# Other places for a table and for the tiles of wo, and 99 operations at other positions of the stored order, in a kernel that mixes dilated attention and a spectral filter

## The chip, the cores and the metric

The kernel runs on one core of one Trainium2 chip. The metric is the device time in microseconds (us); the kernel before takes 453.42 us, the median of three runs (453.15 to 453.45).

## The reference

```python
# x: (1, 2048, 640); 32 heads of 20; 8 taps 2 apart, looking back only
qkv = (x @ wqkv)                                  # split into q, k, v per head
logits = einsum("bhsd,bhswd->bhsw", q, k[taps]) * scale     # masked where s - 2w < 0
a = einsum("bhsw,bhswd->bhsd", softmax(logits), v[taps]) @ wo
b = irfft2(rfft2(x) * (w_r + 1j * w_i), s=(2048, 640))
g = sigmoid((x * gate_w).sum(-1, keepdims=True))
out = g * a + (1 - g) * b
```

## The kernel before

The sequence is cut into 16 blocks of 128 rows, even rows ("xe") and odd rows ("xo") apart. The projection to q, k and v runs in groups of heads. A weight is loaded raw, cast on ACT to its high part and subtracted on DVE or POOL to get the low part, and PE multiplies the parts. The first weights are loaded as `st` tiles by ACT's own DMA queue. The sums (`ev`) go out to a buffer in DRAM (`qkvd`) and come back for attention as `kt`, `q` and `vt` in units called 0a, 0b up to 7b.

`attend` computes one such unit in four steps: `pr` = kt times q (a copy of q is made on ACT into one of three thirds of a PSUM bank, `qbank`, and DVE multiplies with it; some pieces are multiplied on POOL straight from q), a reduction into `L` (the logits, e.g. `L6a`), then maximum `m`, exponential on ACT, sum `s`, reciprocal. After that POOL multiplies `vt` with the weights into `pv`, and DVE reduces that into `o`, which is stored.

The spectral half is a two dimensional Fourier transform by matrix products. `freq(g)` treats one of 16 groups of frequencies in the order 1, 2, 3, 0, 4 to 15. PE makes `u` and `v` from `zc` and the table `bt`; ACT copies v to `vs`; DVE makes `ab` = u + vs and u - vs; PE makes `x` and `z` from ab and the table `mm`. ACT copies x into `P` and writes `X`, a signed copy of x and z, and two DMAs on ACT's queue carry its halves across the partitions into P. POOL multiplies P with the filter `wp` and adds two parts of it; DVE finishes `z`, then makes `s`; PE makes `g` from s, and ACT copies g into `zg`, which the later spatial stage (`oa`, `ob`, `ha`, `hb`) reads. Group 0 is special: it has a table of its own, `tbfirst`, and a second pair `ix`, `iz` instead of the exchange by DMA. The last stage multiplies the attention's output with wo (`woa`, `wob`, output `ya`); a transposed tile is `oTp` in PSUM and `oT` in SBUF. `load_wo` loads wo raw (`wor`), casts it on ACT and subtracts on POOL.

No scheduler orders the work. `Plan.record` collects every operation of every engine; `Plan.order` decodes a stored list of indices (`ORDER`, 99 of whose entries concern us here), takes the operations out one by one in that order, and `Plan.issue` issues them. Since each engine works through its own instructions in that order, an operation that must wait holds all that stands behind it on the same engine, DMA issues on ACT's and SP's queue included. Every instruction is therefore shown at line 385, the line on which the helper executes it, and tiles have to tell them apart.

Where a tile lies is fixed by its tag. `Ring` hands out tags in turn, and a tile with the tag of an earlier one may be written only when that one's readers are done. `x0` to `x7` first hold `st` tiles and then xo; `raw0` to `raw4` the raw weights and later zc, vs, X.

Of the kernel before, what the change touches and what calls it, by code (L numbers as in the profile page):

```python
# [201 lines left out]


ORDER = """
T>t<81poj4|NsC0{{R31`zHT%QmDPk&^9H>y=H*?`Lk%9Gnl%)B_CdQV7rLsIrdLM6sJFoVB8Rk|2U=URH5DLwHy3}>N|I2375U5sNENOZ_r>p;QjNS0Qt^d&3_BFn1BL!{U(U9<aW#`
(4{je$Bsor%a-5-0xjIIz5Bhxq2@_J(ZuU^ngytDZDQ}-t=xl(zWY*>f`~oBV87-{Mb^4R1miDSrW!ct$(P^W^D-my%k>BL--#k$dtRgI1R2eM!0IO6o?xU&oVN(ll5SwBMVENpPvsM&
VX`y5BH+<-e7!dXm4S)sH)6INBza7DP`fU`9t|k`wa4c^oeIq*)7CzRjTY+mf9&=qHQ*h+Q~~C@lecBhmUgi^3s$MljG$M^2A?T>032Y~xgI;PDn0`}JfpXlPl|zc84Qwq<`4=%Gxo}a
8aTyUW$<0lvv}Yi{qWtE5;ndiT9Il;=`-mwYQl}5l>T>2mc)1@SbB472vpebS-0G>xhr1`IH0OO^WWem*}=TuJ*N?b=-d(+YVg*L!??m3Sl>7Ow>k%WopAr_cs>TQ#{0e@C)rMmjvX42
HQ(%xOkCb5Ti|9M&74oX@)~%FC+g&Um>cIj7Th&a$THElCM_Qxh94S8@_R$YuH^AlZ29A62|gtX_GwKt861v*&%|Lj%A~%)Ju4ard*J9-%@(h(=zcz=9{hy8`{2ylZ=~+70?!1ipBf(&
zwb}8-f;L(FVHcuzwYP7?2%s*U{nv&ECs$KBfw^t@z;C&Xf&zSgn_WXO0Ra-A{p=`KSTo&WCxLcHX{frWWSucqtk!hm#2nHJeX5P<a5rX;@Kti_Yl8ko7HnBP?BD0BCR!|nSp+9pO(On  # L210
7C*Q$o$wOs&SmSBdiC|DHG?D8$uS*E_ccd=5LY{i^BiXwbd{r0)D57<l%^E2DaY|53+8~ZxRJddAoRNdJYPz%5Lvh5W}S={Qu`$OJ}cwneg)RxR)(xpZMXtIs%DRMvJ7u?%%!@^1B8h@
(qlVz@tLYv`rnaOHo>WRfe{k*SBQiEnDF!z+o6MsFAJ=(MehAC+OQk;gfj{$D4Y9E8C&GfcpM}t1W|C%hJ#;L!7aan3ZqicP~xB7_Qnrj(tTe<@R?W&V{($jS4EF-5t#TOP0?OuT|3Qa
eIT(hT>jCQrecqER6AALUaUC?)=4v!RW)w9%$6TmkX}rmdZ1<A!<Ce0_LGFT-55A$ndz>!p$dHdxh1>o=3<(6z*KuxX86ZbhMDSB?~D@~6mK>u#>!XP<ORCokbE-Ovd^FevYd6|yTLNh
6LqbJKy?z;o)=#fxd)}q(t!E7s4(3|QOszQKMHHgt&?pyfYSMq-!@LPp=HMQOrhAsZ-JWy-C3Mc^Z`{5!$bngKocKj*>1lOfpe>gL<4DAk0)0!w_E-I8Ix5zA0pAPHAB79wZiA}lY^=h
Std;TST@mvK(Izv+y2xl{ZkLjAJfK%G&=WMvx-dxg6DMA424jO9cS?4TWJptst&`UzGq$ZfJ_rYlV4K31$NLXrgHytE*H`DST?S8Z+_yEBRpdjK2A~uXM4Nj32C4N!P4z2;Hqn$;QEkU
x#r;cod7g-0_+HHSjTx0G?wMOQFZ}koI>bLqzm3R1#oY}9`o)-A1NE;d6CRy2FU=-R;2owOP)Xp5@L{{lo`pBpk%V|R6g=MDVwD`bNH=OjT}S9%<^i$H2}^WSgi-blEMMxNCWOt@KVe#
HqSpv<!^C>%lNmv7RSF7$EOxNC{yKe#`U(Lx+?J!T>!ZP9DRYha-KfY6f?D)z+1)BTY#H0H8P_on~L7A?2-f-TVGlJ$NYiPg`Ivs?eZmoz*1s%9Xd;!3V#C-+$0Brl2%!N#H_A1i{L@S
P#-7P*l5}1Q+W5C%(=qlbU3pZ%otQHBXliSa7Eq92vyz1<`-h2wlnrTN(?T$K{1wyGNT3yESJ?d;(Zw=a_uas{jBg++Q~Nj2jh-_=z=SgoGX(xs<sgT2K8=TN&l`u^j-}yWbYSO(5cEw
hVcGl#lx!tpndKnI3W6}4nYMD+Pk`P27A{L32W`ao5f1Lx*Nb1X()n(JDUZ2O2az;7O<uub@cq%>A*E(_tL!Qq_R=1wNX@G<vau7PJDCp_$;h81hHJ;PIGy_$BYC9!FRj&Q%d@dloNT&
V}(@XS$iJK7_UBeT9exaHe0ZCd>(H!PSGFR8O~kQ=y2V-@rw&$Jg2mnKHs;xrCurTIvRujMxI%zzSsUAbNQyk@KBwL05WxN*Sm)5I2Xq^XZjzH)Ihl#)t51ss6A^!b?3)adQa(X1?V`Q  # L220
wEf(@vgv8sXd>1A(Inx$aDsF9o|pp|HZf+o&w(aEY-(nPPdJX2mvN>(E_fL#$UQPvI|Oa9cnbzr-e$^;-WQD_g83Pq)JF@6puq4=iw_oAzI4h0IpY+hbO=V@zz#KK7T>Y)df*No_7zw#
J`ZNS1m5yd>sTzrvwN&$9|njAQz>w>cl%q7wQZn?8p!=9m>5`9rRfIf_1}m*K9QWX2p$bk-U|1B1Z(^)NFjGTUi*=`v=?z{hl`I|qiO|ofbK~N2V}%VS*t!h=6?gk(z$O~7sEFHmYj%6
MNgL}676SI+-J!42{U}iie@2JyD7wX?tWyweu6+;9xiJSQlECBlw3cU6JNL9Qbq$0tUe_bx^QVlnRQ^tl#ei^!;Uy@((9<|ywE43$z4IgNR)3HBAWp^wA5G)i`pF3l<h}x3OgiJc*rTp
yDIhR4d;b1#P9;B=Fn!{JagvZWQ8Dna+>C8?PWN5+e!O%eKQFD7&UwCI9EJuzf24eM=px5vm)*=iSJQOsoOrV0(&B;X_MREg42C+90%XRnO_)k_RRKzcw`jk&FlJtxyJ@dT+yf~v((s8
-2h}>WX&Km>`JDrIZsB~HyMCyj)w7Emh<Bxtc+@vJ<-~GPXyd<K2@BwUFJSEEbOSLf-}5Tj30C4oH>gKhj@`yM0lgO1I|~8Uz5d)n(Ap~u7*R$VC*4V^uL@BrFYVSXJ!#;GPx$-`iB^*
2MiYfr5xOz@(Hn_ZO=uraJXL7TjCH2Oo22&4b<5GbESU)fMy@w<%JD=kBRvs^7YntD5lPeG0~#A(Y7f~=u1vSN3y;*%B)if3ZHyCNgsIjl_GRnl%27NSP+9t2PA;2H4bS5GyaV=>j*#x
*M~~EY1!7%?esLp+*GX}o-QD6C&^J6=;H8X|6(A(`yZi}Z}faaS0?Gjqv@lj&ep&tv$=yAF_CROwlnc;Gg~`p{^9llwa}e7zb`&fYr`LIz+M4&!D;pBW0~8c-9pQAVK~5|Lst>X_XHJf
BbHYtz@n{+NemE;D#YqvNyi@TUL%=x!c}A)W#~0YXI_9y%G_JmIy7up9F-wz0Ko(;nI?_m?Kd3a(}245c2v@Jf1OP32?$)b@4&S%LtI4Xl7SDnL8i5%lEDj)>G1TqOFDWr8uzjy&O3Nm
d$+wYoEer$Aq-KST1DqGF`N6nbu3i9J1y!73cVHXcW7RCc*0zmf=AnkP~}&rJ5)<G5jD!ivtsQGa!*YrUZ<x(O%YP2uxAQgki#<4cU6)m;~U+_$c%HUxDD2C>6*du+*nLhT21G%FSMTx
F9o90(I?=4__Uh>X7zl2S;|3%g?xk&&ZNy<yz%i{Sl87#;Hq(*dX#-S;0K7k`-=_DNmtn_cWizA<)OfVpjTP3DV~JDA&$35ndX-;RJ~3efGwiJ5Ht%!mBpiuzqzwAm%V<N$YT+%N<y?-  # L230
L$<-n`T;@{9ha=_DU5Caogirb*l5ll(=hVGvPaUVHGn@TTk@(O%Cg>+!F&Z>^a}MWs*HoAIXZ*IGmD&KQ1$s5UlW<f%b`0L6Zo}XxY*ejMiL6wZB3VWksk25LDcc$*m+|kO*MiA5qM!R
E4&I$iUB%e=t-&vI#oE3omS`8qhKNa{&xtjquCoj@gt~4hPP`#R?lah{_Fr2NG)2)6j`)6xWw-bn!#53kreFmg|f%8{Hi9hP;wz{AL5rvcI#V0DymT1c(Kucy<*0`8=s--Bri8zDH~#v
%-FB#M0Qq%ICg_IFP2C48|n56Sm9Um9k2fiPvpqah%)KEUW1~=uV*6=QB*z{Al8lvW9Q;ye=6Tp=v>L79H5IQ5X|z~#8hpnJr+Ga_QrkC4`Rhv7#WXovCK>ybSs8B6l~NOoIP)O5Fr!S
+}fcYgLx<p#v>wbK=gW?vhdCXZVtgKhsHNHj%~Qolp5+lQ(hjj51#p5_1_2~j|^=(cHJD!9j9&qpZdcxvk%!cXv8;;W{9m%oyJFbB38c|mac656_T8#{}Kg@00
"""


# [729 lines left out]
```

## Time and profile before

| | |
|---|---|
| median of three runs | 453.42 us |
| profiled execution | 455.89 us |
| its span on the core | 454.1 us, 7249 instructions |
| mean granted TensorE clock | 0.996 |
| PE, DVE, POOL, ACT busy | 441.2, 409.8, 363.9, 211.9 us |
| moved by DMA | 110.75 MB, mean 244 GB/s |

The span is the time from the first to the last instruction of the profiled execution; 1.79 us of its 455.89 us lie around it. Busy times are those of arithmetic instructions, PE being TensorE's matmuls, PEld its weight loads, DVE VectorE, ACT ScalarE, POOL GpSimd, SP SyncE; ACTq and SPq are the DMA queues that those engines issue to. All times in the rows are counted from the start of the span. A group of like instructions is shown as one row with its start, its length and their number.

### The profile page before, as it was taken

The page shows a single profiled execution, that of the slowest core. Times are in us where ns is not written, and L with a number is a line of the kernel's source. Part 1 is how long each engine was busy: PE and PEld are TensorE (multiplying, and loading weights), DVE is VectorE, ACT ScalarE, POOL GpSimd, SP SyncE. Part 2 cuts the span into 40 slices and gives each one's busy share as a digit, 9 for nine tenths or more (in the row PEclk, how much of TensorE's full clock was granted, in tenths as well). Part 3 has the DMA queues.
Part 4 walks back from the last instruction along what each step waited for, and adds up shares of the span by engine and source line. Part 5 has one row for each costly group of instructions (what it writes and reads, how often), then busy time and mean ns, then how long its engine had stood idle before and what let it go on. Part 6 is the DMA issues. An engine that isn't in the chain of part 4 may idle for free. (4 is left out here: it accounts for less than half of the span.)

```text
span 454.1 us, 7249 instructions
## 1 busy us (share of the span) xinstructions
PE 441.2 (97%) x2440; PEld 391.8 (86%) x2440; DVE 409.8 (90%) x519; ACT 211.9 (47%) x561; POOL 363.9 (80%) x316
## 2 busy tenths in 40 slices
PE   9999999999999999999998989999989999999996
PEld 6888888888889888899886769998877899999996
DVE  4899999899999999999978989999999997899484
ACT  4723165625226463255356666667554655342110
POOL 1158895899899898988977898976899998889810
PEclk9999999999999999999998999999999999999999
DMA  8998999887968979679979778989883331365932
GB/s 312 401 383 268 340 330 377 305 264 237 272 183 272 340 217 316 181 216 320 303 220 294 240 230 250 297 245 320 258 257 105 85 97 54 118 207 134 296 123 87
DMA packets 73956, 110.75 MB, mean 244 GB/s; under 512 B 21296, under 2 KB 50992, under 8 KB 73920
## 3 DMA queue, kind: packets, MB, share of 16 engines
q1 hardware_dynamic: 40192, 69.32, 46.8%
q10 hardware_dynamic: 32816, 36.97, 26.1%
q0 software_dynamic: 912, 4.00, 2.4%
q8 instruction: 19, 0.31, 0.3%
q14 instruction: 17, 0.14, 0.1%
HBM read 72.51 MB, written 32.84 MB: 232 GB/s over the span
## 5 line engine op out<-in xcount | busy, mean ns | idle before, releaser
L385 PE MATMUL qkv<-w,xo 128*128 128x480 f32 (+1 forms) x480 | 110.6, 385 | 0.0
L385 PE MATMUL qkv<-w,xe 128*128 128x480 f32 (+1 forms) x474 | 104.3, 382 | 0.0
L385 PEld LDWEIGHTS qkv<-w,xe 128*128 128x128 f32 x474 | 89.3, 189 | 15.2 <-ACT xe L385 0.9
L385 PEld LDWEIGHTS qkv<-w,xo 128*128 128x128 f32 x480 | 89.7, 189 | 13.8 <-ACT zg L385 0.2
L385 ACT COPY ev<-qkv 128x480 f32<-128x480 f32 x64 | 34.9, 558 | 48.3 <-PE qkv L385 35.9
L385 PE MATMUL woa<-wo,oT 128*128 128x320 f32 x240 | 47.2, 318 | 0.4 <-ACT oT L385 0.4
L385 PE MATMUL wob<-wo,oT 128*128 128x320 f32 x240 | 46.9, 315 | 0.2 <-ACT ya L385 0.2
L385 POOL TENSOR_TENSOR P<-P,wp 128x963 f32<-128x963 f32 (+1 forms) x16 | 35.4, 2212 | 6.6 <-DMA P<-X 4.0
L385 PEld LDWEIGHTS woa<-wo,oT 128*128 128x128 f32 x240 | 37.7, 188 | 1.1 <-ACT oT L385 0.6
L385 PEld LDWEIGHTS wob<-wo,oT 128*128 128x128 f32 x240 | 37.8, 188 | 0.6 <-ACT ya L385 0.4
L385 POOL TENSOR_TENSOR fx<-fx 128x160 f32<-128x160 f32 (+1 forms) x16 | 12.8, 818 | 24.2 <-DMA fc<-in_t_fc 17.1
L385 POOL TENSOR_TENSOR w<-raw,w 128x480 fp32r<-128x480 f32 (+1 forms) x20 | 24.8, 1262 | 5.3 <-ACT w L385 5.3
L385 ACT CAST oT<-oTp 128x384 fp32r<-128x384 f32 (+1 forms) x32 | 13.4, 427 | 30.9 <-PE oTp L385 17.3
L385 PEld LDWEIGHTS g<-mm,s 128*128 128x128 f32 x150 | 21.0, 190 | 7.1 <-ACT zg L385 5.0
L385 PE MATMUL g<-mm,s 128*128 128x128 f32 x150 | 23.5, 280 | 3.1 <-ACT zg L385 3.0
L385 DVE TENSOR_TENSOR oT<-oTp,oT 128x384 fp32r<-128x384 f32 (+1 forms) x32 | 15.2, 485 | 11.0 <-ACT oT L385 10.7
L385 PE MATMUL oa<-gt,zg 128*128 128x161 f32 (+1 forms) x96 | 24.0, 344 | 0.0
L385 PE MATMUL ob<-gt,zg 128*128 128x161 f32 (+1 forms) x96 | 22.0, 344 | 0.0
L385 PE MATMUL u<-bt,zc 128*128 128x240 f32 (+2 forms) x96 | 21.1, 335 | 0.7 <-DVE ab L385 0.7
L385 PE MATMUL v<-bt,zc 128*128 128x240 f32 (+2 forms) x96 | 21.5, 335 | 0.2
L385 DVE TENSOR_TENSOR fx<-fx 128x642 f32<-128x642 f32 (+2 forms) x24 | 19.2, 798 | 0.7
L385 PEld LDWEIGHTS u<-bt,zc 128*128 128x128 f32 x96 | 16.9, 199 | 2.9 <-PE g L385 0.9
...
## 6 DMA issues: line engine op xcount, KB each, us to landing
...
```

Source lines behind the costliest of these rows:

```text
L385: p.dve.memset(w, 0.0)
```

## The change

Three things differ in the code; the rest of the difference is the text of `ORDER`.

```diff
         self.abr, self.Pr, self.s12r, self.Xr = ring("x0", "x1"), ring("x2", "x3"), ring("x4", "x5"), ring("raw3", "raw4")
-        self.p1r = ring("x6")
 
-        self.wor, self.war, self.yar = ring("ya", "w7"), n("w", 7), ring("ya")
+        self.wor, self.war, self.yar = ring("w7", "ya", "raw4"), ring("w0", "w1", "w6", "w2", "w3", "w4", "w5"), ring("ya")
...
         if g == 0:
-            tb = self.one("tbfirst", 1280, tag="x7")
+            tb = self.one("tbfirst", 1280, tag="x6")
             S.dma_start(tb, ins["t_first"])
...
 ORDER = """
-T>t<81poj4|NsC0{{R31`zHT%QmDPk&^9H>y=H*?`Lk%9Gnl%)B_CdQV7rLsIrdLM6sJFoVB8Rk|2U=URH5DLwHy3}>N|I2375U5sNENOZ_r>p;QjNS0Qt^d&3_BFn1BL!{U(U9<aW#`
+T>t<81poj4|NsC0{{R31`zHT%Q|y%^AnXPlHozE}p7FDqEzdbj!3YLaHP#Jsvmhw(>8e8*ToUvR{d?J>oxGWMC!<)DwUB5Ts->b4+5{V0K_?;1afKCrejcFy*&@zSA%k%*KIjNk%RU{$
...
```

The ring p1r had no user. The raw tiles of wo take turns in three places instead of two, one of them (`raw4`) shared with every second X; the split tiles of wo use the same seven places in another sequence. The table of group 0 lies in x6, where xo1 was, and no longer in x7, where xo3 was.

The moved operations lie all over the program. A number behind a tile's name in the rows below tells tiles of one name apart; a minus stands before a row of the kernel before, a plus before a row of the changed one.

On DVE, at the end of attention's unit 7b and the beginning of unit 6a, where the first groups of the frequency stage begin (ab_606 belongs to the first of them, group 1):

```order
 L385 TENSOR_REDUCE o3b_465<-pv3b_467 128x160
+L385 TENSOR_TENSOR pr6a_504<-kt6a,qbank 128x1280
 L385 TENSOR_TENSOR pr6a_505<-kt6a,qbank 128x1280
 L385 TENSOR_REDUCE L6a<-pr6a_505 128x2x8x4
+L385 TENSOR_REDUCE m7b<-L7b 128x32
+L385 TENSOR_REDUCE L6a<-pr6a_504 128x2x8x4
+L385 TENSOR_TENSOR ab_606<-u_605,vs_604 128x321 x2
 L385 TENSOR_REDUCE o7a_478<-pv7a_479 128x160
-L385 TENSOR_TENSOR pr6a_504<-kt6a,qbank 128x1280
-L385 TENSOR_REDUCE m7b<-L7b 128x32
-L385 TENSOR_TENSOR ab_606<-u_605,vs_604 128x321 x2
-L385 TENSOR_REDUCE L6a<-pr6a_504 128x2x8x4
```

The product pr6a_504 stood behind another product, its reduction and o7a, and now stands ahead of them; the maximum of L7b, the reduction of pr6a_504 and ab_606 also come ahead of o7a_478.

On ACT, at the start of the program (st_90 to st_92 are raw first weights, st_85 a tile of x):

```order
 L963 UNCONDITIONAL_BRANCH
 L385 DMA st_90<-in_w 128x482 x2
+L385 ACT_TABLE_LOAD
+L385 CAST xe<-st_85 128x3x128
 L385 DMA st_91<-in_w 128x482
 L385 DMA st_92<-in_w 128x482
 L385 DMA st_91<-in_w 128x482
-L385 ACT_TABLE_LOAD
 L385 CAST w_0_93<-st_90 128x482
-L385 CAST xe<-st_85 128x3x128
 L385 CAST w_1_94<-st_90 128x482
```

Three of the five loads of first weights are issued after the loading of ACT's table and the first cast of x instead of ahead of both.

On ACT, in the frequency stage, around group 3 (P_631 and X_634) and group 1's output (g_0_628):

```order
 L385 CAST wo_333<-wor_339 128x320
 L385 ACTIVATE X_634<-z_633,sign 128x321
-L385 DMA P_631<-X_634 64x642
 L385 COPY zg<-g_0_628 128x48x8
-L385 DMA P_631<-X_634 64x642
+L385 DMA P_631<-X_634 64x642 x2
 L385 COPY vs_653<-v_652 128x321
 L385 COPY P_631<-x_632 128x321
```

The copy into zg stood between the two transfers of P_631 and now stands ahead of both. Later in the stage it goes the other way at some groups: of P_754, P_767 and P_807 the second transfer has moved behind copies that it preceded. On PE one of the six `warmed` matmuls of the start stands between the second and the third of the first products, and a few neighbours in the frequency stage have changed places; on SP the loads of wor and tbfirst, and of some `mm`, `ot` and `ad` tiles, stand elsewhere.

More of the change, by code (lines that the diff above doesn't have):

```diff
@@ L204 @@
 ORDER = """
[L205 to L232, printed above, removed]
@@ L233 @@
-%-FB#M0Qq%ICg_IFP2C48|n56Sm9Um9k2fiPvpqah%)KEUW1~=uV*6=QB*z{Al8lvW9Q;ye=6Tp=v>L79H5IQ5X|z~#8hpnJr+Ga_QrkC4`Rhv7#WXovCK>ybSs8B6l~NOoIP)O5Fr!S
-+}fcYgLx<p#v>wbK=gW?vhdCXZVtgKhsHNHj%~Qolp5+lQ(hjj51#p5_1_2~j|^=(cHJD!9j9&qpZdcxvk%!cXv8;;W{9m%oyJFbB38c|mac656_T8#{}Kg@00
+T>t<81poj4|NsC0{{R31`zHT%Q|y%^AnXPlHozE}p7FDqEzdbj!3YLaHP#Jsvmhw(>8e8*ToUvR{d?J>oxGWMC!<)DwUB5Ts->b4+5{V0K_?;1afKCrejcFy*&@zSA%k%*KIjNk%RU{$
+&te1@wQ~lv8?pKTI1bRnqxn(QtUI+i`}zoUISq?S{{3XzfVoV?<6`YqJIAhsmVdqill&>k*3rNv)S<Lo?fQGD3R&`Hx5)Cxs?wt_eomD4|7%2FIO{3<L;0b!m$?2hI+H-0Btkw643ue#
+)JDx@2+`2o#clcl4_g)72ziBeo#ZAN?&Un?k8Jjl9fKwuieuO3Dg(o&k!*do!R`JSe&j!8n}?A?!YJr|okA0gA0hlH9)ORhOX4?)(cU^ginWR?!)Jq8r-(%si?UN99Hpbw$Lz27%muZ7
@@ new lines @@
+H|}y^%G+`_5BP7*-6)cn9GFj9tYCOK)#goWpppu{zZ^b-y5QUc4l?;3Dd#c83H?5Zd%^=`Q#`AuJY$W4>?q-DdJJ!sB#F@}*ScdUX}f!k@^Y^5bYFvx*sS76i^-BfMp@=dffDvhb1;`r
+pQ!d5-Dfa{&Y|@Hf2ZR97@Oy6O1MIPLOQIXse5CM@?h8z<3UGmpDM-(((4pH?1Cn{1Wpeg5htZsSZ>4)1a<f8=$?J}QA66*{rfEHp>wm|1nvd65PvjX84`}Wy;{ZX*%%F~rYru00gIz_
+g<n>zz|fhohK2p?4v2<F9UoPPw2)UcQZ)AjS5SHie74}x6eA|j=KLClQF216DzIPWg0>;_dOK6y)f?#uM#7iL9+il~_^B(?!L3Z{0%Q70(yrQ4rmPd{=I9vpE>GqXhwKJ?CAQ`ZNxLEI
+%(c=h^<ncqo)8?6Zk}p;ta&BqqW7|9*=ijC6JuwH<bhXyVYKU(mpLZGJEN@rCP0s_%Jkgs^dA`s9fK7L>1RK{Gi4$d9ltWKZ2M>egL(MW-@QlG3iSctv7~gf+Ztu@s@}Ofa4Ff9A;wR`
@@ new lines @@
+<LirhR3-Gk!1Ugltt=w|5bMWP{ndxO=2W?(;>7UgOod&!>BcXv_@2~m62WXYQ}D!|$~}nzpPFP3brtKT!-EcXi@kw{qF6{dKELM39pWWWs?<}JU&3uhR#BW=2a^i2%EVSz&l3&=ncftJ
++yMdiE><wQshdako<&V~b(5oTd&KeFDsLZWz`>rC(IWz5#y*j>PhmbZ16(O9qDVlJd&sx>-A@a-Dpj$ZN`Lu3po$&dP0uOue^1zNgcoK-N2zXC%%<C&YUJDL%FFK|<NSx)j^PWHXPL%K
+8UeQl=(SEEq$gU<W`zf}4MAj(B*DT;SK;h+c9-t<+c+7b@xfns-6UhToHKrtRWy`ivvY}ktSqy%WUnbsAVx4M8pA60?Z>?&iE+=jl~+f$v#yR;WD;LuQ=Itr^L*f+)v&ngLQcCJ9y|c8
+qzjs8i3=k#k(van=!ygLntJ@x5y(t~>beUHOO9}9ZQAbCX+w3^B;D+My5a?;E?S^L4m7?T?yGjwTPd8`E@X={y3RQS7%Nrj5;$3h<(_OoiQXr!07(7{N+WCW-Z#PL1LIGXJ#SZ5hIS{#
@@ new lines @@
+Cxr?=J<(Gm{{_fuvs-H_dUT6mj&KEROSDfwaVz@f6~T0x_-8xf%uup0P_uoapx5;eYMuthCKkZD4Lx*%+g2R0>rfbh`d-ydYoaV^<=8~;04uiCA0?&{;>HFi&=gP}Y2UuE`#@ByZ+oq$
+6V{cH-Wm-o>r;?<C<;g#%18`Oofjqs9#>sct#%V}@xr~<iP-g#Q?Sj<daHiESGB=Q`>8O@9M4hnc!?ZUG7lq(6vES!x-X~&)auC&vg_t#Kvrm9<w+HPVg|-EUn*883Dj?g<1*kyzTrfE
+Z4>AE!GzN{>tokuNJX^Q7WD7HLZQs#dm3muBcSc3$;H3^PulqRZ761uz7ws_{cj#Dv0Fe2u<Ji8&ose0XW-y0{Vfwz1+*44VXPyv#>d{X;cIOs_BVX%v`Xw>SzwsWOHiPbx+;irn99KU
+$ONm@D(D+J0*5Hqc27&!V@7dYc(Qc}*o$_i%f1F@85eVx7bo3{jQXnU_a6-s=+Db@mE~v3-8OGC1LZ4zI0`KN6L93}W-`$Rm1ps&RpFo1Y(e^OmkhbY3HtP)Cfr@VhJM8w!{Y0|BN5oS
@@ new lines @@
+Lvr%lRX9?YUf^bNFK>U78-awoAPwMp9rm^x_XaC(&{D5riwc^fukWz$mI%wkTL*p?W$V*^8^>NBe=?NY``*)5PEzR)fuCUe;5{LSm?=P_zfc0pn2j`D-fw8p$vC96UulL|8?Ms|R2rTK
+_a}NN0feHZ=ajtI#i#bElQc{JwJD%|UE|KmQOz1KCS{GFikBl;5&J9^#q|ErT2}$E*X3!mlcR+*wNiYkIP2~gqcZBR?!1hwucfC%n)Scan0)=PDs6=N71LdAE@S%|m@keLWLE@knm(T?
+iUX5FsxC#?e?G(FhQ9vsuG=u5byQm2SjYeB?DFD)Q<kc$SV5lC`?KKa6k?n{)bkqvd72WjTrRa%z`*&1q#`S<5qg^L1*6WgFg8Iob;5K_3ITeeo%EnkBphD&&}MaWW}+Z80%mHl$}!v!
+Z=vppq_n}HC~J8$U*1d0wZ%omS6sbgHgjN41Y`Xn?VA&i&Ln<5zGeN@{09z`fTpV15@lncIA4rp)cY5=M;AtvUO{An;Rb=~v8a*b>Xo?|Rz>*YvOVM!+HlwgROMA-e<bWr@9%+S_S9yc
@@ new lines @@
+%tX{rUHt;_C^I$?yQR-;k-C?8L2V@U-qe5Vx<OzTN&t4IS-u~^$RP<w33Jwr;l1GLYwA5bAtw5_k*V&w*K^i#89Ee|e$p4joxn7Dt+dYX@Fn)PH8)vl=a_$>g@%#b-(vYRn-mJ37z%yn
+*S<xdAg(KD>x&S*b+Yx`zgvQHO-%PwC>~C@m{Hi0ss>Na4Jx?R2&d4|b*p<XQwXBLDM5mRykw>f)(p~d#1xUq-;3hN*sxi|Po)6L<@CUN$ES={@Ggr^nOBOp2k*Y#cJ<dcS9{Vb;QvS3
+{(+T8)ApILG>>fKaVPJzGmMTacwqUv=Zr+ATwBWpWe0FtmwHfm#@?H92YK;WtnJR(fTVaF)4!qDsQ4UW6S0^sIfY3A&j^%74Y5OWzL>-E6X_O|O!tfX-IdVt(|==E+788I(P`Sgj{dHv
+8?A#Dk+G_Tv@(~_4o#w{H=wqX{&{Cm3Lz%0wYY!5%d#^0EUUD+vpMjP9H7F|CVY3-L=xmt_~{?vr(F>He+TMg+?ZiEI@$3`buD6zud;XvtfjAi9}lINVlkONVlTTAT(jP01?{!qJ~v37
@@ new lines @@
+AZ<fH<ml<rV)8*1R`*#S-E#^0Gw${7{R?Q|vT6WMbkLn+9~s+FalH_Ac((81bhLTt=$@<NEh`8xg8a&10i!`O-aa~2t8t>II`y&R$9sIK`FWD_4OeKR*nk<S*Mq!&!Irf)C4veD@oOLL
+Xhs6;PNZtukHVny*T?fVoDf6z+4C5v<K{Q*?`p1_${@Lc2=-S(xPBT{zAw{qez6b1sxd+Hmb&h}^pBVSD&u(KT&#sK&@Wm=#ue$4bZl+D$XX?tPc0OVvbWi!E`0bReU@-CH;f9Lln<7O
+l)_oJDE3_|h=`=P#||P^YpCR+l>poht<!hX5QyZpUtea0TZ^U24|~Dh5LHuJhxV?G`sk4z+W%Ti-w<{~z-;QgXqZpA8z=HU>icL7+791{?Nb#YUq3lnE#u`q2JeaNNI+J3#tn#!Bs1F!
+<Rv;7$X}e~0MS#esAM7g3Dm8d^FwlarHasq`0Ks}9RJ<wUb{nifz$Lgqyk!#(8H!jt*>iv@s3xDPD0t@g|~i(BCzFmX~;L$Uq_bLc|}{vThwE#Gl4S&>7`}2p|WRH{7SVzXTSC4Nlp^G
@@ L235 @@
+$L8L0abQg7;Cl3+d^HpDgskjEV<fw~CeFNUoTnH5_xdi3(liM7rlvu2MswghL3nriXYTS3n>4HP9pFeW=Wzlh>*nG&#w`-ba?93862S#8)j5C`AC0=*J)};U)n#ScduON}zTSRg644vk
+#Z{yb)p})sF{4tHwX@g$bAlJ5e7rtE|1P}-Fo-DD^BIxuNCK*zUd)?6YSVog$0ER!ux_r|h{uQ`rs?A2c4UE>lR<C`&wF;wDA7WLMEnj6!BVmHgnL|&_0J=HNJ#61YSXM+vh{lSdNZna
+#G{mU=b^7xm!lPHVIb&iahpIV=|ma*bGfT_v#XZG-BQ_6oLmZq&)j;|dFBI@1Da)l=(~QJ{;3f0W0_bFjOjF@kK%zEG<M^Pr>)^E`8PSWWp@iiy)Rd>(nZP!hf(eOEgDygPtlw=|JpQj
+b^
 """
```

## Prediction

> **What bounds the kernel now.** I read the engine totals first, then PE's share by stage, then what PE waits for, and last the timelines of the engines that it waits for.
>
> ```profile
> PE 441.2 (97%) x2440; PEld 391.8 (86%) x2440; DVE 409.8 (90%) x519; ACT 211.9 (47%) x561; POOL 363.9 (80%) x316
> 230.00:240.00 10.00, 9.31 (x48) 7.65 (x46) 8.90 (x9) 7.22 (x22) 7.11 (x9) 1.00 0.85 241
> 240.00:250.00 10.00, 8.57 (x37) 7.37 (x38) 8.26 (x16) 5.83 (x19) 7.17 (x7) 0.83 0.96 303
> 250.00:260.00 10.00, 9.24 (x51) 7.62 (x50) 9.91 (x14) 6.82 (x20) 8.16 (x9) 1.00 0.81 250
> 260.00:270.00 10.00, 8.05 (x48) 6.72 (x47) 8.31 (x15) 5.54 (x17) 9.84 (x8) 1.00 0.65 184
> 350.00:410.00 60.00, 60.00 (x380) 55.11 (x380) 53.68 (x76) 29.61 (x77) 52.68 (x44) 1.00 0.35 106
> ```
>
> The first row is the page's, the others are stretches with PE, PEld, DVE, ACT and POOL busy in that order, then the granted clock. PE is busy 97% of the span, so time can only be won where it idles or runs slow. It idles between 230 and 270 us (0.69 + 1.43 + 0.76 + 1.95 = 4.83 us), and there is the one stretch whose clock is below 1.00. From 350 to 410 us it is busy throughout: whatever has been won or lost by then is carried along.
>
> ```profile
> 238.74 0.57 PE L385 MATMUL v<-bt,zc 128*128 128x240 f32 x2
> 241.33 0.78 PE L385 MATMUL x<-ab,mm 128*128 128x321 f32 x2 [2.02 <-DVE ab L385]
> 252.82 0.71 PE L385 MATMUL g<-mm,s 128*128 128x128 f32 x4 [0.76 <-ACT zg L385]
> 262.99 0.81 PE L385 MATMUL z<-ab,mm 128*128 128x321 f32 x2 [1.24 <-DVE t L385]
> 336.79 0.94 PE L385 MATMUL g<-mm,s 128*128 128x128 f32 x6 [1.03 <-ACT zg L385]
> 239.11:242.52 3.41, 1.39 (x6) 1.00 0.99 345
> 242.52:245.93 3.41, 3.41 (x13) 0.50 0.87 250
> 245.93:249.34 3.41, 3.32 (x20) 1.00 0.97 305
> 259.58:262.99 3.41, 2.17 (x15) 1.00 0.28 69
> 262.99:266.40 3.41, 2.71 (x13) 1.00 0.82 240
> ```
>
> PE's timeline gives its longest idle pieces (start, duration, and in brackets idle time and releaser); the rows with colons are stretches of PE alone. The longest, 2.02 us, is the second filter group's x transform waiting for ab. In the 3.41 us that hold it PE was busy 1.39; for the next 3.41 us the clock was half. A stretch with 1.24 us idle (2.17 busy) was followed by full clock.
>
> **The change part by part.** Why ab is late stands in DVE's and ACT's timelines.
>
> ```profile
> 224.05 1.48 DVE L385 TENSOR_TENSOR pr6a<-kt6a,qbank 128x1280 f32<-128x1280 f32 x1
> 226.97 1.48 DVE L385 TENSOR_REDUCE o7a<-pv7a 128x160 f32<-128x1280 f32 x1
> 231.00 1.49 DVE L385 TENSOR_TENSOR pr6a<-kt6a,qbank 128x1280 f32<-128x1280 f32 x1 [2.56 <-ACT qbank L385]
> 232.41 0.41 DVE L385 TENSOR_REDUCE m7b<-L7b 128x32 f32<-128x256 f32 x1
> 232.73 0.88 DVE L385 TENSOR_TENSOR ab<-u,vs 128x321 f32<-128x321 f32 x2
> 240.70 0.88 DVE L385 TENSOR_TENSOR ab<-u,vs 128x321 f32<-128x321 f32 x2
> 245.71 0.89 DVE L385 TENSOR_TENSOR ab<-u,vs 128x321 f32<-128x321 f32 x2 [1.61 <-PE u L385]
> 228.37 2.20 ACTq L385 DMA_DIRECT2D vt6a<-qkvd  x1
> 230.67 0.30 ACT L385 COPY qbank<-q6b 128x160 f32<-128x160 f32 x1 [2.73 <-POOL pr6a L385]
> 230.90 0.42 ACT L385 COPY vs<-v 128x321 f32<-128x321 f32 x1
> ```
>
> *DVE's order at pr6a.* DVE idles 2.56 us because its fourth row here, pr6a_504, stands behind pr6a_505, L6a and o7a, and by then needs a copy that ACT made at 230.67, after an issue of vt6a that held ACT 2.20 us. Changed, pr6a_504 stands first, so that it needs only an older copy, and m7b, L6a and ab come ahead of o7a. I count from the 224.05 at which DVE is free. The two pr6a take until 226.9 (1.4 each, start to start), one L6a until 228.35, m7b 0.4, the other L6a until 230.2. The first ab then waits for vs (230.90 + 0.42 = 231.32): 1.15 us instead of 2.56. Itself (0.85) and the five long operations that stand between it and the second ab (o7a, pr6a, L6a, o7a, L6a, at 1.4) bring that one to 239.2 instead of 240.70: 1.5 us earlier. PE's x followed 0.63 behind it, so it starts at 239.83, PE is free at 239.31, and the wait of 2.02 becomes some 0.5. Behind ab on DVE are z and pr6b, which move with it.
>
> *The clock.* With 0.5 us idle in a stretch, less than the 1.24 that kept full clock, I take the half clock as gone: 3.41 us at 0.50 are 1.7 us of work. DVE goes along: its third ab, at 245.71, waited 1.61 us for PE's u, which comes 1.5 + 1.7 = 3.2 earlier, and its own queue is 1.5 earlier with 1.61 of waiting to spare, 3.1 in all. Bounds: 1.5 if the clock dips anyway, 3.2 if all holds.
>
> A rule of the Trainium skill, "TensorE: Matmul & The Clock Gate", Part 1: a free-running window of about 3.4 us decides, and the array falls to half clock after at least one idle window. The rows agree on the length (3.41) but not on the condition, since 2.02 us of idleness in a window was followed by the dip.
>
> *ACT's order in the frequency stage.*
>
> ```profile
> 251.47 0.47 ACTq L385 DMA_DIRECT2D P<-X  x1
> 252.28 0.48 ACT L385 COPY zg<-g 128x384 f32<-128x384 f32 x1 [0.89 <-DVE o7a L385]
> 256.33 1.48 DVE L385 TENSOR_TENSOR pr6b<-kt6b,qbank 128x1280 f32<-128x1280 f32 x1
> 335.20 1.12 ACTq L385 DMA_DIRECT2D P<-X  x2
> 336.36 0.37 ACT L385 COPY zg<-g 128x256 f32<-128x256 f32 x1 [1.23 <-POOL pr5b L385]
> 343.42 0.75 POOL L385 TENSOR_TENSOR P<-P 128x321 f32<-128x321 f32 x1
> 346.98 0.71 PE L385 MATMUL g<-mm,s 128*128 128x128 f32 x4 [0.57 <-ACT zg L385]
> ```
>
> At 252 the copy of zg is put ahead of both P transfers instead of between them, which frees 0.5 to 0.7 of PE's 0.76. I cost it at nothing: in 250 to 260 DVE is busy 9.91 of 10, so PE meets DVE's ab and s a little further on with the shift that DVE has. If DVE had room, it would be worth -0.7. At 336 zg is put between two transfers of P that used to precede it: -0.6 there, while the second transfer is issued 0.4 later. That transfer feeds POOL's last P (done 344.2), which is late for DVE's z and PE's last g, at 346.98 with 0.57 of waiting. So it can return as +0.4, and I take 0, between -0.6 and +0.4. The other moved copies (P_794, P_754, ya, L5a) change what lands while POOL is in pr5b; 0.
>
> *The moves on SP, POOL and DVE up to 230 us* (pr0, pr1, pr7, fx, weight stores, loads of raw wo): 0. PE has no wait there after 8 us that the view of its waits shows, and its matmuls cover them; uncovered, one swap of two DVE operations costs 1.4.
>
> *The places.* The table of the special group lies where xo1 was, and SP can load it when that is read for the last time, 3 us earlier; its first reader is the x transform at 253.85, some 35 us after either landing: 0. Three places for raw wo instead of two let the last casts run sooner; the X that shares raw4 waits for a POOL operation that is done before: 0, or 0.5 if the sharing holds an X transfer back by one issue (0.47). The removed ring p1r was in no use.
>
> *The start.*
>
> ```profile
> 0.74 3.45 ACTq L385 DMA_DIRECT2D st<-in_w  x5
> 4.22 1.28 ACT L385 ACT_TABLE_LOAD   x1 [4.22 <-DMA st<-in_w]
> 8.40 0.59 ACT L385 CAST w<-st 128x482 fp32r<-128x482 f32 x1 [0.86 <-DMA st<-in_w]
> 8.90 1.03 ACT L385 CAST xe<-st 128x384 fp32r<-128x384 f32 x2
> 3.88 3.42 PE L385 MATMUL qkv<-st,st 128*128 128x482 f32 x4
> 6.57 5.68 PE L385 MATMUL qkv<-w,xe 128*128 128x482 f32 x22
> ```
>
> ACT issues five weight loads in 3.45 us, then loads its table. Changed, it issues two, loads the table, casts xe once, and only then issues the other three, some 1.6 to 2.1 us later each. The first casts gain: the table load no longer ends at 5.50. The third weight, awaited by the cast at 8.40, shares its queue with the two before, and lands late by 0 to 0.3 by my estimate; the cast of xe behind it ends about 0.7 ahead of its use. One of six warming matmuls (0.42 us of PE) now stands behind two real products. Sum +0.2, between -0.1 and +0.4.
>
> **Sum.** -1.5 - 1.7 + 0.2 = -3.0. Against the profiled execution's own 455.89 us (span 454.1, 1.79 around it) that is 452.9. The median of the runs is 453.42, 2.47 below the profiled one; the difference carries over, so 450.4.
>
> **The rivals.**
>
> *The clock dips anyway.* The stretches that decide may lie otherwise against the program in the timed runs, which then have no dip to lose (the 2.47 us between the profiled and the timed executions has room for 1.7), or 0.5 us of idleness adds up with another gap. By the rule of the Trainium skill the gap was not the cause of the dip, and the dip would stay. For it: the gap's part of the window is known for one execution only. Against it: the dip stands right behind the only long gap. Then only DVE's 1.5 is won: 453.42 - 1.5 = 451.9. The same number comes out where POOL (9.84 of 10 in 260 to 270) hands half of the shift back.
>
> *DVE waits anyway: no difference.* The issue of vt6a is what really holds ACT; if in the new order it holds ACT 1.4 us longer, vs comes at 232.7 and ab is as late as before. Against it: what the issue waits behind is a transfer that is issued at the same place. 453.2.
>
> *The start turns against it: slower.* The three late weight loads: if they land late by the whole 2.1 us of their issue, the 0.7 us ahead of the xe cast turn into 1.4 of PE waiting, and such a gap in the first stretches can keep PE at half clock for one more window, +1.7 (3.41 at half). Alone that is +3.1, and the kernel is slower only from where it exceeds the gain at 241: it decides when both fall on one execution and the clock at 242 dips too, 3.1 - 1.5 = +1.6, 455.0. For it: the cast at 8.40 waited 0.86 for its load already. Against it: the five loads share one queue, which an earlier issue does not make faster.
>
> **How the numbers follow.** Likeliest case 0.60: 450.4, its own range 449.0 (with the -0.7 at 252 and -0.6 at 336) to 451.3 (with +0.4 at the start and at 346). Clock dips anyway, or half is handed back: 0.18, 451.9, up to 452.5. No difference: 0.09. Slower: 0.13. A measurement of this kernel tells 0.2%, 0.9 us, from no change; the first two cases are faster by more than that, so faster 0.78, same 0.09, slower 0.13. The range of 449.0 to 452.6 takes in the first two cases and a part of the third.
>
> **What would show it.** In the profile of the changed kernel: ab on DVE behind L6a, waiting for vs some 1.2 us near 231; PE's x at 239.8 with about 0.5 of idleness instead of 2.02; no stretch near 242 with 0.50; PE's z, at 262.99 before, near 260; the end of the span 3 us earlier. Wrong would be: a wait for ab above 1.5 us, a clock of 0.50 anywhere past 10 us, casts of the third and fourth weight past 9.2 and 10.9, or a last g later than 344.4.

## The result and the profile after

The changed kernel takes 457.13 us, the median of 9 runs (455.2 to 460.82), against 453.42 us for the kernel before in the same runs: a ratio of 1.0078, 95% interval 1.005 to 1.0107. It is slower by 0.8% where 0.7% faster was forecast. (The ratio is not the quotient of the two medians; it comes with the interval.) Its profiled execution took 458.24 us, with a span of 456.0; that of before took 455.89 and 454.1.

PE's stretches in the changed kernel (PE busy, granted clock, DMA share, GB/s):

```profile
0.00:10.00 10.00, 7.79 (x27) 1.00 0.83 306
230.00:240.00 10.00, 10.00 (x52) 1.00 0.96 291
240.00:250.00 10.00, 8.83 (x47) 1.00 0.92 248
250.00:260.00 10.00, 8.75 (x47) 1.00 0.89 272
260.00:270.00 10.00, 8.91 (x56) 1.00 0.74 229
310.00:320.00 10.00, 7.96 (x48) 0.94 0.80 233
320.00:330.00 10.00, 9.80 (x60) 0.89 0.83 224
```

And its longest idle pieces from 230 us on, from PE's timeline:

```profile
241.25 0.78 PE L385 MATMUL x<-ab,mm 128*128 128x321 f32 x2 [0.66 <-DVE ab L385]
261.46 0.81 PE L385 MATMUL z<-ab,mm 128*128 128x321 f32 x2 [0.39 <-DVE t L385]
317.45 3.28 PE L385 MATMUL wob<-wo,oT 128*128 128x320 f32 x15 [2.04 <-ACT ya L385]
338.52 0.94 PE L385 MATMUL g<-mm,s 128*128 128x128 f32 x6 [0.69 <-ACT zg L385]
349.19 0.71 PE L385 MATMUL g<-mm,s 128*128 128x128 f32 x4 [0.57 <-ACT zg L385]
```

The forecast gain is there: x waits 0.66 us for ab instead of 2.02, and no dip of the clock follows at 242. PE's start of that x is nevertheless no earlier (241.25, before 241.33), because the kernel came to it late: PE is 1.28 us behind before at 239 us. At 261.46 PE is 1.53 ahead of before (262.99). Then a wait of 2.04 us stands at 317, where before had none, and behind it the clock is below 1.00 in the last two stretches shown: 3.41 us ran at half clock from 318.79. That dip belongs to this execution; six of the nine have a mean clock of 0.999 or 1.000, the one of 457.13 us among them. The last g, at 346.98 before, starts at 349.19.

Two places thus cost: the start, and the place of a store on SP.

**The start.** ACT's timeline:

```profile
1.67 1.28 ACT L385 ACT_TABLE_LOAD   x1 [1.67 <-PEq L956]
3.78 2.50 ACTq L385 DMA_DIRECT2D st<-in_w  x3
6.32 1.09 ACT L385 CAST w<-st 128x482 fp32r<-128x482 f32 x2 [2.03 <-DMA st<-in_w]
9.95 0.60 ACT L385 CAST w<-st 128x482 fp32r<-128x482 f32 x1 [2.03 <-DMA st<-in_w]
11.94 0.60 ACT L385 CAST w<-st 128x482 fp32r<-128x482 f32 x1 [0.45 <-DMA st<-in_w]
```

The cast of the third weight comes at 9.95 instead of 8.40, that of the fourth at 11.94 instead of 10.11:

```profile
10.11 0.60 ACT L385 CAST w<-st 128x482 fp32r<-128x482 f32 x1 [0.18 <-DMA st<-in_w]
```

This row is of before. Each lies behind the marks that the prediction set (9.2 and 10.9). SP's queue shows a reason. The first row is that of before, the second that of the changed kernel:

```profile
0.75 5.07 SPq L385 DMA_DIRECT2D st<-in_xE  x6
```

```profile
0.75 3.34 SPq L385 DMA_DIRECT2D st<-in_xE  x6
```

SP's six loads of x (up to 448 KB each) are out in 3.34 us instead of 5.07, and ACT's three late weight loads, issued from 3.78 on, now stand behind all of them. In before the third weight was issued at 1.67, when three of the six were out.

**The store.** SP and ACT near 310 us, in the timeline of before and then in that of the changed kernel:

```profile
307.62 0.32 SPq L385 DMA_DIRECT2D ad<-ya  x1
315.58 0.53 ACT L385 ACTIVATE ya<-woa,g 128x320 f32<-128x320 f32 x1 [1.20 <-PE woa L385]
```

```profile
309.79 0.32 SPq L385 DMA_DIRECT2D ot<-od  x1
310.67 0.37 SPq L385 DMA_DIRECT2D od<-o6a  x1
311.13 0.46 SPq L385 DMA_DIRECT2D ad<-ya  x1
316.87 0.53 ACT L385 ACTIVATE ya<-woa,g 128x320 f32<-128x320 f32 x1 [4.13 <-DMA ad<-ya]
```

All tiles ya lie in one place, so ACT may write the next one only when the store of the last has landed. Before, the store was issued as soon as ACT had made ya. Now it stands behind a load that waits for PE's oTp and behind a store that waits for DVE's o6a. ACT stands 4.13 us, and PE's wob, which needs the bank that ACT is to empty, 2.04.

### The profile page after: what moved, and what is told of

Same layout as the page of the kernel before. It is cut to its first block, busy times and chain, and to the rows that moved or that the text cites. A ratio compares the mean times of both kernels' runs of the same rounds, so it can differ in the third digit from the quotient of the medians.

```text
span 456.0 us, 7247 instructions
## 1 busy us (share of the span) xinstructions
PE 441.1 (97%) x2440; PEld 391.0 (86%) x2440; DVE 409.5 (90%) x519; ACT 212.1 (47%) x561; POOL 364.6 (80%) x316
## 5 line engine op out<-in xcount | busy, mean ns | idle before, releaser
L385 ACT CAST w<-raw 128x480 fp32r<-128x480 f32 (+1 forms) x30 | 17.2, 595 | 14.0 <-DMA raw<-in_wqkv 10.5
L385 PE MATMUL u<-bt,zc 128*128 128x240 f32 (+2 forms) x96 | 20.0, 322 | 0.7 <-DVE ab L385 0.7
```

The source lines that it names most:

```text
L385: p.dve.memset(w, 0.0)
```

## Experiments

Seventeen runs follow, one of them of before itself, mostly of 12 executions each (6 of the start alone, 4 of the slowest kernel). Each is compared with the kernel before on the same chip, where the median of before was 453.49 to 454.49; so kernels of different chips are to be compared by their ratios and not by their medians. Ratios below 1 are faster than before.

| kernel | median us | ratio to before, 95% interval |
|---|---|---|
| changed kernel | 457.13 | 1.0078 (1.005 to 1.0107) |
| it, store put back | 456.66 | 1.0046 (1.0026 to 1.0067) |
| it, start put back | 455.90 | 1.0031 (1.0014 to 1.0048) |
| it, both put back | 454.03 | 1.0004 (0.9985 to 1.0023) |
| before, start alone | 456.20 | 1.0059 (1.0038 to 1.0081) |
| before, store alone | 454.41 | 1.0020 (1.0002 to 1.0038) |
| before, pr6a alone | 454.12 | 0.9999 (0.9981 to 1.0017) |
| before, two places alone | 453.22 | 0.9993 (0.9980 to 1.0007) |
| before, pr6a, mm1, wp12 | 452.99 | 0.9967 (0.9948 to 0.9985) |

### The kernel before once more

> The kernel before, unchanged, to read the granted clock and the span of each of its executions. Theory A (a half clock window follows a long idle piece only where both fall together in the grid of windows): mean clocks of 1.000 in most of its executions and of 0.996 in a few, the latter some 1.7 us longer; 453.4. Theory B (the dip at 242 belongs to this order in every execution): 0.996 in all of them.

454.52 us, ratio 1.0006 (0.9989 to 1.0022). In 35 other executions of before, on the chip of this and the next three runs, the mean clock was 1.000 in 22 and at most 0.996 in 3; the 3 took 455.24 to 456.66 us, where the median of all is 453.84. Its profiled execution was again one with the dip. Stretches of PE, first in this profile, then in that of another kernel whose order is that of before at this place (the run of the store alone):

```profile
239.00:242.10 3.10, 1.15 (x7) 1.00 1.03 277
242.10:246.00 3.90, 3.90 (x13) 0.61 0.84 291
```

```profile
238.00:242.00 4.00, 2.13 (x12) 1.00 0.91 251
242.00:246.00 4.00, 4.00 (x22) 1.00 1.00 344
```

In the first, PE idles 1.95 us of 3.10 and then runs at a mean clock of 0.61; in the second it idles 1.87 of 4.00 and the clock stays at 1.00. Theory A holds: the dip belongs to an execution, not to this order. On the chips of all experiments together, 12 of 145 executions of before had a mean clock of at most 0.996. Both profiled ones had it; whether profiling favours the dip is open.

The Trainium skill says of the warm-up, in "TensorE: Matmul & The Clock Gate", Part 1: the window is free-running, and where a program falls in it varies from run to run. These rows agree, here in the middle of a kernel. They do not agree with its condition of at least one idle window for the fall to half clock.

The traces show what decides. They hold each change of the granted clock, and in all 19 profiles these changes lie whole multiples of 3.413 us apart, on a grid that lies otherwise against the program in each execution. On that grid, first two windows of the changed kernel around its dip, then two of the run of the store alone:

```profile
315.38:318.79 3.41, 1.36 (x10) 1.00 0.87 340
318.79:322.20 3.41, 3.41 (x16) 0.50 0.35 78
```

```profile
237.50:240.91 3.41, 2.50 (x14) 1.00 0.86 243
240.91:244.32 3.41, 2.45 (x13) 1.00 0.99 350
```

Between the first rise of the clock and the last 5 us, every window of the grid in which PE was busy for 1.49 us or less was followed by half clock, and none in which it was busy for 1.95 or more; of two with 1.57 and 1.58 one was. In the run of the store alone like idleness fell into two windows, and PE was busy for 2.45 us or more in both.

### Put back the store, the start, and both

The store, in the changed kernel (the start is put back by the reverse of the difference in the section on the change):

```diff
  DMA wp_745<-in_ws 128x1284
+ DMA ad<-ya_834 128x640
  DMA ot_844<-od_65 128x640
  DMA od_66<-o6a_510 128x4x80
- DMA ad<-ya_834 128x640
```

> The changed kernel with one DMA put back on SP: the store of ya_834 again ahead of the load ot_844 and the store of o6a_510. Theory A (that store, issued 4.8 us later against the work around it, holds ACT's next ya for 4.13 us and PE's wob for 2.04 us): the wait of 2.04 at 317 goes, and with it the dip behind it; 2.0 us less where the clock did not dip, so 454.4, and no execution above 456. Theory B (POOL and DVE are so close behind that another wait takes its place at once): 456.5 or more.

> The changed kernel with the start of before: ACT issues five weight loads ahead of its table load, six warming matmuls ahead of the first products, DVE's first two operations as before. Theory A (the start costs 0.6 to 0.8, and a load of f 0.4 more behind it): 1.0 us less than the changed kernel, 456.0. Theory B (the start is taken in by waits further on): no difference, 457.

> The changed kernel with both put back, the start and the store of ya_834. Theory A (the two are independent and are the whole loss): 453.2, no slower than before, and 1.5 us better than before where before's clock does not dip, if the gain at pr6a holds. Theory B (something else of the 99 moves costs too): above 454.

456.66, 455.90 and 454.03 us. With the store alone put back the wait at 317 is gone from the profile, yet executions reach 457.7, and the ratio falls only from 1.0078 to 1.0046, 1.5 us: theory A's size was wrong there. With the start alone put back the profile keeps a wait of 1.83 us for ya and a dip behind it. With both put back the ratio is 1.0004, 3.4 us are gone, and the kernel can't be told from before. The two are nearly the whole loss. But no gain is left over, although theory A promised 1.5 from the order at pr6a. Inside the span this kernel is 0.3 us ahead of before, and the time around the span is 2.2 us here against 1.77.

### The start alone, the store alone, the places alone, in the kernel before

The first is the difference on ACT's start, with the matmul `warmed` and DVE's first subtraction for xe that go with it, and nothing else. In the second only one store moves; in the third only the code changes, and the order is that of before:

```diff
  DMA wp_745<-in_ws 128x1284
- DMA ad<-ya_834 128x640
  DMA ot_844<-od_65 128x640
  DMA od_66<-o6a_510 128x4x80
+ DMA ad<-ya_834 128x640
```

```diff
-        self.wor, self.war, self.yar = ring("ya", "w7"), n("w", 7), ring("ya")
+        self.wor, self.war, self.yar = ring("w7", "ya", "raw4"), ring("w0", "w1", "w6", "w2", "w3", "w4", "w5"), ring("ya")
...
-            tb = self.one("tbfirst", 1280, tag="x7")
+            tb = self.one("tbfirst", 1280, tag="x6")
```

> The kernel before with the start alone as in the changed kernel. Theory A: PE loses 0.6 in the first 20 us, since the three late loads land 1.5 to 1.9 later, and some of it again at the loads of f near 210: 0.6 to 1.2 more than before. Theory B (waits further on take it in): no difference.

456.20 us, 2.7 us above before in the same runs: over twice what was expected. From the timeline of this kernel, the late weight loads on ACT's queue, the cast of the third weight, and the loads of x on SP's queue:

```profile
3.70 2.69 ACTq L385 DMA_DIRECT2D st<-in_w  x3
10.69 0.59 ACT L385 CAST w<-st 128x482 fp32r<-128x482 f32 x1 [2.64 <-DMA st<-in_w]
0.75 3.26 SPq L385 DMA_DIRECT2D st<-in_xE  x6
```

The third weight is cast at 10.69, 2.29 us later than before. It landed at 10.67, right behind two loads of x of 448 KB on SP's queue (8.74 and 10.48). In this profile PE is 1.53 us behind before at 18 us, 2.13 at 66 and 2.56 from 147 to 230 us. The profiles scatter in this: with the same start the changed kernel is 0.61 behind at 18 us and 1.36 at 230, and the run of the store alone, which starts like before, is 0.74 behind at both. What makes the lateness grow is not shown. That the waits further on do not take it in is shown by the timed executions, 2.7 us.

> The kernel before with the store of ya_834 alone put behind the store of o6a_510 on SP. Theory A (the store's place is what holds ACT's next ya): it is issued at 312.2 instead of 307.62, lands near 317.9, and PE's wob waits 1.5 to 2 us; in some executions a dip follows. 1.5 to 2.5 us more than before. Theory B (the wait needs the shift that the changed kernel has at that point): under 0.5 more.

454.41 us, 0.9 more than before: between the two theories. With the start alone (0.59% and 0.20%) it makes 0.79%, the loss of the changed kernel being 0.78%. In this profile the store, issued at 309.8, lands 4.3 us later, and PE starts wob only some 0.5 later for it. In the changed kernel the store took 5.65 us, in before at its old place 5.86; what sets this is not shown.

> The kernel before with two of the three changes of places alone, in the old order: tbfirst in x6, and the split tiles of wo in the sequence w0, w1, w6, w2 to w5. Theory A (the places cost nothing inside the span): no difference from before, and 1.77 us around the span as before if the 0.43 that the changed kernel has more there belongs to the order, 2.2 if to the places. Theory B (tbfirst's earlier load crowds the loads of wp_601 and mm): up to 0.5 more.

453.22 us, ratio 0.9993: these two places cost nothing here. The time around the span was 1.85 us, against 1.77 in before. The third change, that of the raw tiles of wo, was not run in the old order.

### A start between the two

```diff
  DMA st_91<-in_w 128x482
  DMA st_92<-in_w 128x482
+ ACT_TABLE_LOAD
+ CAST xe<-st_85 128x3x128
  DMA st_91<-in_w 128x482
- ACT_TABLE_LOAD
  CAST w_0_93<-st_90 128x482
- CAST xe<-st_85 128x3x128
```

> The kernel before with a start between the two: ACT issues four weight loads, then loads its table, casts xe once and issues the fifth load. Theory A (what costs in the changed start is that the third and fourth weight load are issued behind the x loads of SP; a table load in the time in which ACT waits for the first weight costs nothing): third and fourth weight land as before, 8.4 and 10.1; no difference, or up to 0.5 less. Theory B (the table load ahead of any weight load is what costs): 1.5 or more above before.

453.16 us, ratio 0.9991 (0.9972 to 1.0009): no difference. ACT's and SP's rows:

```profile
2.64 1.28 ACT L385 ACT_TABLE_LOAD   x1 [2.64 <-issue]
8.59 0.60 ACT L385 CAST w<-st 128x482 fp32r<-128x482 f32 x1 [1.55 <-DMA st<-in_w]
0.75 5.50 SPq L385 DMA_DIRECT2D st<-in_xE  x6
```

The table load is early here too and harmless. That leaves the late issue of the third and fourth weight load, behind the loads of x, as what costs. The moves of the matmul `warmed` and of DVE's first subtraction, which the start alone had and this kernel has not, are not ruled out by a run of their own; but the 2.64 us that ACT waited for the third weight there end with its landing.

### The order at pr6a alone

In the kernel before, DVE's rows alone:

```diff
+ TENSOR_TENSOR pr6a_504<-kt6a,qbank 128x1280
  TENSOR_TENSOR pr6a_505<-kt6a,qbank 128x1280
  TENSOR_REDUCE L6a<-pr6a_505 128x2x8x4
+ TENSOR_REDUCE m7b<-L7b 128x32
+ TENSOR_REDUCE L6a<-pr6a_504 128x2x8x4
+ TENSOR_TENSOR ab_606<-u_605,vs_604 128x321 x2
  TENSOR_REDUCE o7a_478<-pv7a_479 128x160
- TENSOR_TENSOR pr6a_504<-kt6a,qbank 128x1280
- TENSOR_REDUCE m7b<-L7b 128x32
- TENSOR_TENSOR ab_606<-u_605,vs_604 128x321 x2
- TENSOR_REDUCE L6a<-pr6a_504 128x2x8x4
```

> The kernel before with DVE's order at pr6a alone as in the changed kernel (pr6a_504 first, both L6a, m7b and ab_606 ahead of o7a_478). Theory A (the 1.5 us are won at 241, but most executions of before have no dip to lose, and from 316 us on the loads of wp and the P transfers hand back over 1 us): x waits 0.7 for ab instead of 2.02, and the time is 0.3 to 1.0 less than before. Theory B (what the prediction summed up): 3 us less, 450.8.

454.12 us, ratio 0.9999 (0.9981 to 1.0017): no gain at all. DVE and PE in this kernel:

```profile
231.49 0.89 DVE L385 TENSOR_TENSOR ab<-u,vs 128x321 f32<-128x321 f32 x2 [1.31 <-ACT vs L385]
239.69 0.89 DVE L385 TENSOR_TENSOR ab<-u,vs 128x321 f32<-128x321 f32 x2 [0.34 <-issue]
235.04 0.78 PE L385 MATMUL x<-ab,mm 128*128 128x321 f32 x2 [1.24 <-DMA mm<-in_t_mm]
240.50 0.70 PE L385 MATMUL x<-ab,mm 128*128 128x321 f32 x2
```

DVE does what was worked out: the first ab waits 1.31, and the second starts at 239.69. The second x has no wait at all. But the first x now waits 1.24 us for its table mm1. That load is issued only when the place it goes to, that of a tile ev, has been stored. It was issued at 228.69 and landed at 234.91, in before at 229.20 and 233.56; the load of vt6a, which landed behind it in before (235.24), landed just ahead of it here (234.75). So in this profile a wait of 2.02 became one of 1.24 in front of it.

### mm1 earlier, and then wp12 earlier

mm1 goes to x7, which is free since tbfirst lies in x6, and its load stands behind tbfirst's:

```diff
-                self.mm = self.mdr.next(f"mm{g}", 3, 320)
+                self.mm = self.mdr.next(f"mm{g}", 3, 320) if g > 1 else self.one("mm1", 3, 320, tag="x7")
...
  DMA tbfirst<-in_t_first 128x1280
+ DMA mm_600<-in_t_mm 128x960
```

> The kernel before with DVE's order at pr6a as in the changed kernel (as in the run of that alone) and, besides, mm1 in x7 (tbfirst in x6), with its load right behind tbfirst's on SP, so that it no longer waits for the store of an ev tile and lands some 10 us sooner. Theory A (without mm1's late landing the 1.5 us at 241 show): x waits for no DMA near 235, PE idles 1 us less between 230 and 270 than with pr6a's order alone, and the time is 0.7 to 1.2 less, 453.0. Theory B (DVE and POOL hand the rest back whatever happens at 235): no difference from pr6a alone.

453.81 us, ratio 0.9995 (0.9976 to 1.0015). No wait for mm1 is left, and still nothing is won. Further on, this profile has (PE, DVE, SP):

```profile
319.78 0.81 PE L385 MATMUL z<-ab,mm 128*128 128x321 f32 x2 [1.03 <-DVE s L385]
318.44 0.50 DVE L385 TENSOR_TENSOR z<-z,wp 128x321 f32<-128x321 f32 x1 [1.35 <-ACT X L385]
307.88 0.32 SPq L385 DMA_DIRECT2D ot<-od  x1
308.56 0.37 SPq L385 DMA_DIRECT2D od<-o6a  x1
309.85 0.33 SPq L385 DMA_DIRECT2D mm<-in_t_mm  x1
310.27 4.66 SPq L385 DMA_DIRECT2D wp<-in_ws  x2
```

DVE's z waits 1.35 us. The profile names X, which ACT had long made; what came last was the filter wp12, landing at 318.32. Its place was free at 307.45, but its load stood in SP's queue behind three others until 310.27. Moved ahead of them:

```diff
+ DMA wp_758<-in_ws 128x1284
  DMA ot_844<-od_65 128x640
  DMA od_66<-o6a_510 128x4x80
  DMA mm_771<-in_t_mm 128x960
- DMA wp_758<-in_ws 128x1284
```

> The kernel before with DVE's order at pr6a, mm1 in x7 with its early load, and the load of wp12 put ahead of ot8 and the store of o6a_510 on SP. Theory A (wp12's landing is where the gain is handed back): wp12 is issued near 307.6 instead of 310.27 and lands near 315.5; DVE's z12 does not wait 1.35 for it, PE's z14 not 1.03; 0.7 to 1.0 less than without that move, 453.0. Theory B (DVE and POOL are as late anyway, 9.5 of 10 busy): the wait of PE moves on to a g, no difference.

452.99 us, against 454.49 for before in the same runs: ratio 0.9967 (0.9948 to 0.9985). This is the one kernel of all whose interval lies below 1. Its before is the slowest of the samples of before, whose other medians are 453.42 to 453.99.

```profile
307.62 0.33 SPq L385 DMA_DIRECT2D wp<-in_ws  x1
317.15 0.49 DVE L385 TENSOR_TENSOR z<-z,wp 128x321 f32<-128x321 f32 x1
```

DVE's z no longer waits, and from 310 to 352 PE is busy 39.38 us instead of 38.36. Two more runs tell whose gain it is:

> The kernel before with the load of wp12 alone put ahead of ot8 and the store of o6a_510 on SP. Theory A (wp12 matters only once PE arrives earlier): no difference from before. Theory B (wp12's place is the gain by itself): 1 us less.

> The kernel before with DVE's order at pr6a and wp12's early load, mm1 as before. Theory A (x1 waits 1.2 for mm1, but DVE's second ab is won all the same, so most of the gain remains): 0.5 to 1.0 less than before. Theory B (mm1's wait takes the gain): no difference.

453.76 us, ratio 0.9993 (0.9970 to 1.0016), and 453.88, 0.9988 (0.9963 to 1.0014). wp12's place alone does nothing that can be told, and without mm1 there is no gain that can be told either. Only the three together show one. That each removes the wait that shows once the one before it is gone is a reading of three profiles, and not shown. The intervals with and without mm1's early load overlap, and mm1's and wp12's loads were not run without the order at pr6a. And the wait for mm1 is not in every execution: in the profile of pr6a and wp12, with mm1 as before, mm1 landed at 233.53 and the first x has no wait.

```profile
234.18 0.71 PE L385 MATMUL x<-ab,mm 128*128 128x321 f32 x2
```

### Further combinations

The last kernel with the start between the two besides:

> The same with the middle start (four weight loads, table load, first cast of xe, fifth load). Theory A: both add, 452.5, 1 us less than before. Theory B: no difference from before.

453.97 us, ratio 0.9988 (0.9975 to 1.0001). The middle start adds nothing. This kernel has all three changes of the last one, and its interval reaches 1: the gain was not seen a second time.

With start and store put back, ACT's later moves put back too (first as it is, then with mm1 in x7):

```diff
- DMA P_754<-X_757 64x642
+ DMA P_754<-X_757 64x642 x2
  COPY P_754<-x_755 128x321
  COPY zg<-g_0_751 128x48x8
...
- DMA P_754<-X_757 64x642
```

> The changed kernel with the start and the store of ya_834 put back, and with ACT's order from group 11 on as before (the second transfers of P_754, P_767 and P_807, the copies of P_794 and zg of group 12, the exponential of L5a, the loads vt5b and q4b: eight operations). Theory A (these moves hand back 0.8 to 1.1 us between 310 and 352): PE is busy some 39.2 of the 42 us there instead of 38.26, and the time is 0.8 less than with the two put back. Theory B (what is handed back there is the shift itself, which meets loads of wp that are no earlier): no difference.

> The same as the kernel with the start, the store and ACT's late order put back, and mm1 in x7 with its load behind tbfirst's. Theory A: both gains add, 0.7 to 1.0 below that one and 1 us below before. Theory B: no difference.

453.84 and 454.54 us, ratios 1.0010 (0.9990 to 1.0029) and 1.0011 (0.9991 to 1.0030). Theory A fell: ACT's late order put back left PE busy 37.72 of the 42 us from 310 to 352, not more than the 38.26 without. Those moves are not where the gain went.

With start and store put back, the places of wo put back too, by the reverse of their line above:

> The changed kernel with the start and the store of ya_834 put back, and with the places of wo as before (raw wo in two places, split tiles in w0 to w6 in sequence); the 96 other moves and tbfirst's place stay. Theory A (the order is what lengthens the time around the span): 2.2 us around the span and 454.0, as with the two put back. Theory B (the places of wo do it): 1.8 around the span and 453.6.

480.80 us, ratio 1.0581. Only the places of wo were put back here, and PE waits 24.52 us at one place, for mm1:

```profile
258.50 1.41 PE L385 MATMUL x<-ab,mm 128*128 128x321 f32 x2 [24.52 <-DMA mm<-in_t_mm]
206.71 0.39 SPq L385 DMA_DIRECT2D od<-o3a  x1
243.63 0.35 SPq L385 DMA_DIRECT2D wor<-in_wo  x1
```

With two places SP stands from 206.71 to 243.63 at the load of a raw wo tile whose place is not free, and everything behind it on the queue, mm1 among it, stands too. The load waits for POOL's reading of an earlier raw tile, so it is the third place that it lacks; the sequence of the split tiles, which this run put back too, was not tested apart. Without the new places of wo the changed order is 5.8% slower than before.

## Why the prediction was wrong

- **The start** was the term "+0.2, between -0.1 and +0.4". It measured +2.7 alone. The step that failed: "the third weight ... lands late by 0 to 0.3", argued from ACT's queue alone. It landed 2.29 us late in the run of the start alone and 1.55 in the profile of the changed kernel, behind loads of x that SP now issued ahead of it. The rival with the chance of 0.13 had the late landing, though not this reason, but was slower than before only with a dip of the clock besides; the lateness alone was enough.
- **The store** has no term in the sum: the "0" for the moves on SP is headed "up to 230 us", and what moves on SP near 310 us, the store of ya_834 among it, was put at nothing without a reason. It was put behind an operation that waits for DVE, and its landing is what the next ya waits for. That was 2.04 us in the profile. By the ratios it is worth 0.9 us put into before, 1.5 put back alone and 1.2 put back besides the start.
- **The clock**, -1.7, was right for the profiled execution and no term of the median: 3 of 35 executions of before had a mean clock as low as the profiled one. Its working, by the idle time in a stretch of 3.41 us, agrees with the windows shown above. The prediction carried the 2.47 us between the profiled and the timed executions over to the changed kernel, though it had named the dip as a possible part of them.
- **DVE's order at pr6a**, -1.5, was right in place, and 1.0 in size: in the kernel with that order alone the second ab starts at 239.69 (239.2 worked out, 240.70 in before). In the changed kernel PE's wait is 0.66 (0.5 worked out). No median shows it by itself. The prediction asked what is late next only for DVE's own chain, not for the loads that PE and DVE would meet earlier: PE then waits for mm1 in two of the seven profiles that have this order and mm1 in its old place, and DVE for wp12 in the two with mm1 early and wp12's load in its old place (1.35 and 0.53 us). How much of the 1.0 each of these takes stays open. (The "fourth row" of the prediction's text is the third of the rows above it.)
- **ACT's order in the frequency stage**: 0. The moves from group 11 on cost nothing that can be told (ratio with them put back 1.0010, without 1.0004); that at 252 was not run by itself.
- **The places**: 0, as measured for two of the three in the old order. The kernels with the new places of raw wo have 2.2 us around the span, where the prediction carried over 1.79; that is 0.4 of the loss. That the places make SP's new order possible was not seen.

Three things stay open. The time around the span is 2.2 us with the changed places of raw wo and 1.77 to 1.85 without; the runs tie these 0.4 us to those places but do not tell how. Whether the store's cost, 0.9 to 1.5 us, differs with the order around it can't be told. And where the gain at pr6a goes is read from single profiles, which differ among themselves.
